# Two chained networks on one core: rounds of 384 + 384 rows and seven block products in both

## The chip, the cores and the metric

One core of a Trainium2 chip runs the whole program. The metric is device time in microseconds (us), launch to end. The engines are named as in the profile: PE (TensorE, matrix products), DVE (VectorE), ACT (ScalarE), POOL (GpSimd), SP (SyncE, which issues the DMAs).

## What is computed

Sparse attention, then two feed-forward networks one after the other. Weights arrive as 64-bit floats, the rest as 32-bit ones; the result has 1536 x 512 elements of 32 bits.

```python
# attention: 2 batches, 8 heads, 768 rows, 64 per head; a row sees 8 global and 96 local columns
attn = softmax(scale * q @ k.T + bias, kept columns only) @ v
x = attn as 1536 rows (2 batches of 768) x 512
h = x @ w_in1                                  # 512 x 2048
g = where(h >= 1, h, where(h <= -1, 0, (h + 1) ** 2 / 4))
x = g @ w_out1                                 # 2048 x 512
h = x @ w_in2
return maximum(0.01 * h, h) @ w_out2
```

## The kernel before

**Precision.** Each 32-bit operand of a product is kept as two parts, hi and lo, each in a format that PE takes at full rate. A product of two operands is three matmuls: hi hi, hi lo, lo hi. A copy (L253, L255) makes hi, a subtraction (L259, L261) makes lo.

**Weights.** Each network's 2048 hidden units are 16 chunks of 128. `job` (L460) brings one chunk of `w_in` (o = 0) or `w_out` (o = 1), 64 conversions in all: a DMA of 64-bit words, then s0 (L481, L483), s01 (L487), s1 (L491), s11 (L495), s2 (L499), s3 (L502), which build the 32-bit number, then s4 and s5, which split it into one of the weight places.

**Order of work.** Nothing is written in order by hand. `add` records an operation with its possible engines, its cost on each, a due time and what it waits for; `Schedule.run` (L96) then picks, for each engine, the ready operation that is due first, with buffers handed out from rings. The due times are the terms in `DUE` (L1138), one number for each kind of operation. Its rules count here: an operation that DVE or POOL may take goes to whichever is free, and neither begins an operation without PSUM while the other has one. PE runs what is ready, and before the first rows of the attention are done it runs dummy matmuls (L410).

**First network** (`step`, L779). The chunks go in three groups of 2, 7 and 7. The first group runs in six units of 256 rows, in between the attention, as soon as their rows are there. The others run in three units of 512 rows each. A step is one chunk for one unit: 12 matmuls for the hidden values (L796), the activation on ACT, DVE and POOL (L803 to L818, then hi and lo), 12 matmuls of the output (L858). The output's sums over the chunks of a group stay in PSUM, four banks for 512 rows; at the group's end they are copied into `part` in SBUF, or added to it (L897). After the last group the sums are split into hi and lo, in `x`, as the second network's input. `x_sums` (L941) makes four differences of its quarters, which the block products need.

**Second network** (`two`, L975). Chunks go in eight pairs. For the first 1024 rows, taken as 512 + 512, the hidden values of a pair are a product of 2 x 2 blocks, and they are done with seven block products (L990) instead of eight: two sums of weight blocks more (`sums`, L531, operations at L544), a copy of one bank into another, and two additions between banks (L1035, L1038), each of which stands between two products on PE. The last 512 rows are done directly (L1057). The output of each pair (L1072) is added to `part` bank by bank (L897, in the last pair L915), and then goes out.

PSUM has eight banks. Two word buffers (`wd_r`) and four to eight weight places for each kind let the conversions run ahead. `late` (L1090) frees the attention's buffers when it is done.

Of the kernel before, what the change touches and what calls it, by code (L numbers as in the profile page):

```python
# [205 lines left out]
def emit(tc, q, k, v, n_global, n_local, w_in1, w_out1, w_in2, w_out2, out, narrow):  # L206
# [63 lines left out]
    x = [const.tile([P, 2, KD, UM], F32R, name=f"x{u}") for u in range(NT // UM)]  # L270
    part = [const.tile([P, KD, UM], F32, name=f"part{r}") for r in range(2)] + [None]
# [5 lines left out]
    g_r = ring(const, "g", GN, [P, 2, UM], F32R)  # L277
    t_r = ring(const, "t", 2, [P, UM], F32)
# [36 lines left out]
    units = PASSES[0]  # L315
# [6 lines left out]
    for s, (m, g, u, f, first, last) in enumerate(seq):  # L322
        c = (u[1] - u[0]) * 10.15
        if m == 0 and g == 0 and u != units[-1]:
            after = quads(units[units.index(u) + 1])
            if first:
                seg = GROUPS[0] * c + len(after) * due_["ATT"]
                for i in after:
                    t_att[i] = z + seg * (i - after[0] + 0.5) / len(after)
            c += len(after) * due_["ATT"] / GROUPS[0]  # L330
        t_hid.append(z)
        z += c
    t_hid.append(z)

    NJ = KF // 2
    t_two = []
    z -= due_["TWO"]
    for j in range(NJ):
        for c in (90 * 227, 48 * 227):
            t_two.append(z)  # L340
            z += c
    t_two += [z, z + 48 * 227]
# [107 lines left out]
    for s, e in enumerate(seq):  # L450
        first_use.setdefault(e[0] * KF + e[3], s)
    NC = 2 * KF
    def due_of(c):
        return t_hid[first_use[c]] if c < KF else t_two[(c - KF) // 2 * 2]
# [5 lines left out]
    def job(c, o, prev):  # L460

        m, f = divmod(c, KF)
        due = due_of(c) + o * due_["OUTLAG"] - due_["JLEAD"] - (due_["JTWO"] if m and not o else 0)
# [55 lines left out]
        e2 = add(both(DM), s5, due + due_["s5"], [e1], gives=[] if m and not o else [Dd], late=LATE("s5"))  # L519
        if m and not o:  # L520
            words[f] = Dd, e2
            if f % 2:
                sums(f // 2, due)
# [7 lines left out]
    def sums(j, due):  # L531


        (Da, ea), (Db, eb) = words.pop(2 * j), words.pop(2 * j + 1)
# [41 lines left out]
    def quad(i):  # L576
# [8 lines left out]
        u, ti = divmod(Tt, UM // P)  # L585
# [111 lines left out]
        hi = x[u][:, 0, pp, ti * P:(ti + 1) * P]  # L697
        lo = x[u][:, 1, pp, ti * P:(ti + 1) * P]
# [70 lines left out]
    last_g = [len(GROUPS) - 1, NJ - 1]  # L769
    out_op, fin_op, x2_op, acc = {}, {}, {}, {}  # L770
    last_s = {(e[0] * KF + e[3]): s for s, e in enumerate(seq)}

# [6 lines left out]
    def step(s):  # L779
        m, g, u, f, first, last = seq[s]  # L780
        n = u[1] - u[0]
        r, c0 = divmod(u[0], UM)
        c = m * KF + f
# [3 lines left out]
        if s + 2 < NS:  # L787
            do = t_hid[s + 2] + per_ * due_["half"]
        else:
            do = d + 2.5 * per_  # L790
        wi, wo = w_t[c, 0], w_t[c, 1]
# [8 lines left out]
        def a1(e):  # L800
            t, h = Tt.tile[:, 0:n], Hb.tile[:, 0:n]
            if m == 0:
                A.activation(out=t, in_=h, func=AF.Relu, bias=half, scale=0.5)  # L803
            else:
                A.activation(out=t, in_=h, func=AF.Copy, scale=0.01)

        def a2a(e):

            t = Tt.tile[:, 0:n]
            if e == ACT:  # L810
                A.square(out=t, in_=t)  # L811
            else:
                (V if e == DVE else GP).tensor_tensor(out=t, in0=t, in1=t, op=ALU.mult)

        def a2(e):
            t, h = Tt.tile[:, 0:n], Hb.tile[:, 0:n]
            if m == 0:
                V.scalar_tensor_tensor(out=t, in0=h, scalar=1.0, in1=t, op0=ALU.max, op1=ALU.min)  # L818
            else:
                V.tensor_tensor(out=t, in0=t, in1=h, op=ALU.max)  # L820

        def a3(e):
            copy(e, Gt.tile[:, 0, 0:n], Tt.tile[:, 0:n])

        def a4(e):
            sub(e, Gt.tile[:, 1, 0:n], Tt.tile[:, 0:n], Gt.tile.bitcast(F32)[:, 0, 0:n])

        if m == 0:
            xs = [x_op.get(i) for i in range(u[0] // P * NQ, u[1] // P * NQ)]
        else:  # L830
            xs = [o for rr in range(u[0], u[1], 256) for o in x2_op[rr]]
        fin = s == last_s[c]
        o1 = add({PE: 12 * (n / 2.4 + 13.5)}, hid, d, [w_op[c, 0]] + (o_tb[1] if s < 3 else []) + xs + line("h"), takes=[Hs, Hb],
                 gives=[wi] if fin else [])
        o2 = add({ACT: act(n) + (107 if m == 0 else 0)}, a1, d + per_ / 2 + due_["a"], [o1] + line("a"), takes=[Tt])
        if m == 0:
            o2 = add({ACT: act(n, False), POOL: pool_tt(n), DVE: dve(n)}, a2a, d + per_ / 2 + 200 + due_["a"], [o2], late=LATE("a2"))
        o3 = add({DVE: dve(n)}, a2, d + per_ / 2 + 400 + due_["a"], [o2], gives=[Hb, Hs], ps=True)
        o4 = add({ACT: act(n, False), DVE: dve(n, True)}, a3, do - 2.4 * n - 500, [o3] + line("g"), takes=[Gt], late=LATE("a3"))
        chain.update(h=o1, a=o2, g=o4)  # L840
        o5 = add(both(n), a4, do - 1.3 * n - 300, [o4], gives=[Tt], late=LATE("a4"))

        nb = KD * n // 512 if m == 0 else n // P
        if first:
            acc[m, g, u] = [Slot(banks) for _ in range(nb)]
        bk = acc[m, g, u]
        nk = 512 // n if m == 0 else 1
        prev = out_op.get((m, g, u)) or [None] * nb
        now_ = []
        for cb in range(nb):  # L850
            def mm(e, cb=cb):
                o = bk[cb].tile
                for z in range(nk):
                    for a, b in ((0, 0), (0, 1), (1, 0)):
                        st, sp_ = (first and a + b + z == 0), (last and a == 1 and z == nk - 1)
                        if m == 0:
                            cc = cb * nk + z
                            T.matmul(out=o[:, z * n:(z + 1) * n], lhsT=wo.tile[:, a, cc * P:(cc + 1) * P],  # L858
                                     rhs=Gt.tile[:, b, 0:n], start=st, stop=sp_)
                        else:  # L860
                            T.matmul(out=o, lhsT=Gt.tile[:, b, cb * P:(cb + 1) * P], rhs=wo.tile[:, a, :],
                                     start=st, stop=sp_)
            pr = do + cb * 10
            gives = []
            if cb == nb - 1:
                gives = [Gt] + ([wo] if fin else [])
            o = add({PE: 3 * nk * (n / 2.4 + 13.5) if m == 0 else 681}, mm, pr, [o5, w_op[c, 1], prev[cb]] + now_[-1:] + line("o"), takes=[bk[cb]] if first else [],
                    gives=gives)
            now_.append(o)
        out_op[m, g, u] = now_  # L870
        if first:
            acc_op[m, g, u] = now_
        chain["o"] = now_[-1]
        if last:
            x2_op.setdefault(u[0], [])
            for cb in range(nb):
                finish(m, g, u, cb, bk[cb], now_[cb], do, nk)

    def finish(m, g, u, cb, B_, after, d, nk):
        n = u[1] - u[0]  # L880
        r, c0 = divmod(u[0], UM)
        if m == 0:
            sl = (slice(None), slice(cb * nk, (cb + 1) * nk), slice(c0, c0 + n))
        else:
            sl = (slice(None), c0 // P + cb)
        keys = [(m, rr, cb * nk + z) for z in range(nk) for rr in range(u[0], u[1], 256)] if m == 0 else \
            [(m, u[0] + cb * P, 0)]

        def ac():
            a = B_.tile  # L890
            return a.rearrange("p (k n) -> p k n", k=nk) if m == 0 else a

        def f0(e):
            copy(e, part[r][sl], ac())

        def f1(e):
            V.tensor_tensor(out=part[r][sl], in0=ac(), in1=part[r][sl], op=ALU.add)  # L897

        if g == 0:

            before = list(x2_op.get(("r", r), [])) if m else [o_late if r == 2 else None]
            o = add({ACT: act(512), DVE: dve(512)}, f0, d + 600 + cb, [after] + before, gives=[B_], ps=True)
            for kk in keys:
                fin_op[kk] = o
            return
        if m and g == last_g[m]:
# [377 lines left out]
```

## Time and profile before

| what | value |
|---|---|
| median of 3 runs | 612.18 us (612.14 to 613.44) |
| the profiled execution | 611.8 us |
| its span in the trace | 610.0 us |
| mean granted TensorE clock, share of full speed | 0.996 |
| PE busy | 601.5 us, 99% |
| DVE busy | 471.4 us, 77% |
| ACT busy | 351.6 us, 58% |
| POOL busy | 193.4 us, 32% |

The span is the stretch that the trace covers; the rest of the execution's time lies around it. Busy times are sums of instructions. A matmul's recorded duration includes its way through the array, so that neighbours overlap and a busy PE need not be at its peak; the distance from one start to the next tells more. DVE's recorded instructions overlap a little too.

### The profile page before, as it was taken

What the parts mean: (1) busy time and instruction counts of PE and PEld (TensorE: products, weight loads), DVE (VectorE), ACT (ScalarE), POOL (GpSimd) and SP (SyncE); (2) the same over time, 40 slices, a digit from 0 to 9 for tenths busy, and PEclk for the clock granted to TensorE, in tenths of its full rate; (3) what the DMA queues carried; (4) which work ended last, traced back from release to release, by engine and by line L of the source; (5) the groups of instructions that cost most, each with busy time, mean ns of one, the idle gap of its engine ahead of it and who ended that gap; (6) DMA issues with size and microseconds to landing.
All of it is one profiled execution on the core that took longest, in us unless ns stands there. A gap on an engine that the chain in (4) does not pass through costs nothing.

```text
span 610.0 us, 9623 instructions
## 1 busy us (share of the span) xinstructions
PE 601.5 (99%) x3398; PEld 506.4 (83%) x3398; DVE 471.4 (77%) x1044; ACT 351.6 (58%) x753; POOL 193.4 (32%) x244
## 2 busy tenths in 40 slices
PE   9999999999999999999999999999999999999995
PEld 7889999988888888888888888888888888788884
DVE  6999999999946897623488999249994889678663
ACT  6999999787534576434447457235652366336300
POOL 5666846223200121100111163004530484328200
PEclk9999999999999999999999999999999999999998
DMA  9857523334411334200012131201222113200014
GB/s 206 196 124 178 123 53 86 109 124 134 140 34 35 103 104 138 70 0 1 0 38 66 36 104 36 69 0 70 60 79 69 70 35 105 69 1 0 2 67 146
DMA packets 61809, 46.98 MB, mean 77 GB/s; under 512 B 39608, under 2 KB 56248, under 8 KB 61752
## 3 DMA queue, kind: packets, MB, share of 16 engines
q1 hardware_dynamic: 61744, 46.28, 26.8%
q8 instruction: 29, 0.48, 0.3%
q14 instruction: 28, 0.23, 0.2%
q10 hardware_dynamic: 8, 0.00, 0.0%
HBM read 43.12 MB, written 3.15 MB: 76 GB/s over the span
## 4 chain that ended last, share of the span: by engine, by line


## 5 line engine op out<-in xcount | busy, mean ns | idle before, releaser
L858 PE MATMUL bank<-g,w 128*128 128x512 f32 (+1 forms) x648 | 141.4, 367 | 0.0
L796 PE MATMUL bank<-x,w 128*128 128x512 f32 (+1 forms) x648 | 140.5, 367 | 0.0
L858 PEld LDWEIGHTS bank<-g,w 128*128 128x128 f32 x648 | 113.0, 188 | 20.1 <-issue 0.3
L796 PEld LDWEIGHTS bank<-x,w 128*128 128x128 f32 x648 | 112.3, 188 | 19.7 <-issue 0.2
L897 DVE TENSOR_TENSOR part<-bank,part 128x512 f32<-128x512 f32 x96 | 63.0, 683 | 34.4 <-PE bank L1072 28.3
L1072 PE MATMUL bank<-w,g 128*128 128x512 f32 x312 | 81.3, 389 | 0.0
L502 POOL TENSOR_TENSOR wd<-wd,wr 128x512 int32<-128x512 int32 x32 | 45.8, 1434 | 111.5 <-DVE wd L495 62.9
L253 ACT CAST g<-t 128x512 fp32r<-128x512 f32 (+1 forms) x67 | 39.5, 590 | 56.6 <-PE bank L858 30.5
L1072 PE MATMUL bank<-w,w 128*128 128x512 f32 x264 | 69.6, 389 | 0.0
L1072 PEld LDWEIGHTS bank<-w,g 128*128 128x128 f32 x312 | 58.6, 188 | 12.1
L1072 PEld LDWEIGHTS bank<-w,w 128*128 128x128 f32 x264 | 49.6, 188 | 10.3
L803 ACT ACTIVATE t<-bank,half 128x512 f32<-128x512 f32 (+1 forms) x54 | 34.6, 640 | 40.1 <-PE bank L796 37.0
L253 ACT CAST w<-wd 128x512 fp32r<-128x512 f32 x64 | 39.6, 621 | 27.0 <-DVE wd L502 9.2
L818 DVE SCALAR_TENSOR_TENSOR t<-bank,t 128x512 f32<-128x512 f32 (+1 forms) x54 | 33.7, 625 | 25.8 <-ACT t L811 25.5
L259 DVE TENSOR_TENSOR g<-t,g 128x512 fp32r<-128x512 f32 (+1 forms) x58 | 41.4, 718 | 15.1 <-ACT g L253 14.8
L499 ACT ACTIVATE wr<-raw 128x512 int32<-128x512 uint32 x64 | 43.1, 675 | 8.9 <-DVE wd L502 7.2
L495 DVE SCALAR_TENSOR_TENSOR wd<-raw,wd 128x512 int32<-128x512 int32 x64 | 47.6, 754 | 0.5
L990 PE MATMUL bank<-x,w 128*128 128x512 f32 x192 | 47.2, 389 | 0.0
L657 ACT ACTIVATE sm<-sm,st 128x256 f32<-128x256 f32 (+1 forms) x96 | 46.6, 499 | 0.4 <-DVE st L648 0.3
L672 POOL TENSOR_SCALAR sm<-sm,st 128x256 f32<-128x256 f32 (+1 forms) x78 | 37.8, 501 | 26.4 <-DVE st L663 21.2
L1057 PE MATMUL bank<-x,w 128*128 128x512 f32 x192 | 45.0, 389 | 0.0
L259 DVE TENSOR_TENSOR w<-wd,w 128x512 fp32r<-128x512 f32 x55 | 37.6, 695 | 7.7 <-ACT w L253 6.9
(117 smaller groups left out, 921.7 us busy)
## 6 DMA issues: line engine op xcount, KB each, us to landing
raw<-in_moe_w_in_dram SPq DMA_DIRECT2D x32, 512.0 KB, 3.8
raw<-in_moe_w_out_dram SPq DMA_DIRECT2D x32, 512.0 KB, 3.4
kd<-in_k_dram SPq DMA_DIRECT2D x24, 128.0 KB, 3.9
qd<-in_q_dram SPq DMA_DIRECT2D x24, 128.0 KB, 3.9
vd<-in_v_dram SPq DMA_DIRECT2D x12, 256.0 KB, 4.1
out_dram<-part SPq DMA_DIRECT2D x11, 256.0 KB, 2.2
out_dram<-part SPq DMA_DIRECT2D x2, 128.0 KB, 3.3
vg<-in_v_dram SPq DMA_DIRECT2D x2, 64.0 KB, 4.8
```

The costliest lines, as they stand in the source:

```text
L253: A.copy(out=out_, in_=in_)
L259: V.tensor_tensor(out=out_, in0=a, in1=b, op=ALU.subtract)
L495: V.scalar_tensor_tensor(out=Dd.tile, in0=hl()[0], scalar=-0x40000000, in1=Dd.tile, op0=ALU.bitwise_and, op1=ALU.bitwise_or)
L499: A.activation(out=Rr.tile, in_=hl()[1], func=AF.Copy, scale=2.0 ** -29)
L502: (V if e == DVE else GP).tensor_tensor(out=Dd.tile, in0=Dd.tile, in1=Rr.tile, op=ALU.add)
L657: A.activation(out=Sm.tile[:, a, 0:W], in_=Sm.tile[:, a, 0:W], func=AF.Exp, scale=-1.0, bias=St.tile[:, 0, a:a + 1], accum_out=St.tile[:, ...
L796: T.matmul(out=Hb.tile[:, 0:n], lhsT=wi.tile[:, a, kk * P:(kk + 1) * P], rhs=x[r][:, b, kk, c0:c0 + n], start=(kk == 0 and a + b == 0), st ...
L858: T.matmul(out=o[:, z * n:(z + 1) * n], lhsT=wo.tile[:, a, cc * P:(cc + 1) * P], rhs=Gt.tile[:, b, 0:n], start=st, stop=sp_)
L897: V.tensor_tensor(out=part[r][sl], in0=ac(), in1=part[r][sl], op=ALU.add)
L990: T.matmul(out=bank.tile, lhsT=w.tile[:, a, (2 * z + kk) * P:(2 * z + kk + 1) * P], rhs=xx()[:, b, kx + kk, :], start=st and kk == 0 and a ...
L1057: T.matmul(out=Hb.tile, lhsT=w.tile[:, a, kk * P:(kk + 1) * P], rhs=x[2][:, b, kk, :], start=(kk == 0 and a + b == 0), stop=(kk == KD - 1 ...
L1072: T.matmul(out=Bo.tile, lhsT=Gt[z, r].tile[:, b, cb * P:(cb + 1) * P], rhs=wo[z].tile[:, a, :], start=(z == 0 and a + b == 0), stop=(z == ...
```

## The change

Both networks now work in rounds of 768 rows, one batch, taken as 384 + 384. The first network keeps only its first two chunks (`SOLO`) as steps of 256 rows beside the attention. Its other 14 chunks are seven pairs: the first (`DIRECT`) is done directly, the other six in seven block products, as are all eight pairs of the second network, for both batches. Each pair's output is added to `part` by itself. For the first network's products the differences of quarters are made from the attention's output (`t_sums` with m = 0, which first adds hi and lo in two temporary tiles); weight sums are made for all pairs but the first. The weight places become 4 + 2 + 2 for `w_in` and 4 for `w_out`, the tiles of activations 7 of 384. All due times in `DUE` are other numbers. The diff's core:

```diff
-GROUPS = (2, 7, 7)
-SMALL = tuple((r, r + 256) for r in range(0, 1536, 256))
-LARGE = tuple((r, r + 512) for r in range(0, 1536, 512))
-PASSES = (SMALL, LARGE, LARGE)
+SOLO = 2
+PASSES = tuple((r, r + 256) for r in range(0, 1536, 256))
+UB, UH = 768, 384
 RING = 4
-MORE = 4
+MORE = 2
+MORE2 = 2
+MOREG = 3
+DIRECT = 1
...
+    seq = [(u, f) for u in PASSES for f in range(SOLO)]
...
+    PAIRS = [(0, f) for f in range(SOLO, KF, 2)] + [(1, f) for f in range(0, KF, 2)]
+    NJ = len(PAIRS)
...
+    def t_sums(m, q, kk, got, d):
...
+        if m == 0:
+            w0 = add(both(UB), lambda e: whole(e, kk), d - 200, [o_late] + got + x_rd[q] + t_last)
+            w2 = add(both(UB), lambda e: whole(e, k2), d - 100, [w0])
+            a0, b0, a2, b2 = [w0], [w0], [w2], [w2]
+        else:
+            a0, b0, a2, b2 = got
+        t1 = add(both(UH), c_((kk, 0), (kk, 1), (kk, 0)), d, a0 + b0)
+        t3 = add(both(UH), c_((kk, 1), (k2, 1), (kk, 1)), d + 100, [t1] + b2)
+        t2 = add(both(UH), c_((k2, 1), (k2, 1), (kk, 0)), d + 200, [t3])
+        t4 = add(both(UH), c_((k2, 0), (k2, 0), (k2, 1)), d + 300, [t2] + a2)
+        rd = x_rd[q] if m == 0 else []
+        us_ = [parts((kk, 0), lambda h: x[q][:, h, kk, hb[1]], UH, t1, 0, "t1", rd),
+               parts((kk, 1), lambda h: xt[q][1][:, h, kk], UH, t3, 100, "t3"),
+               parts((k2, 1), lambda h: xt[q][0][:, h, kk], UH, t2, 200, "t2"),
+               parts((k2, 0), lambda h: xt[q][2][:, h, kk], UH, t4, 300, "t4")]
...
+    def two(j, q):
+        m, f = PAIRS[j]
...
+                    o1 = add({PE: 2 * c6}, hid, dd, w1 + xs(y, 0) + (xs(y, 2) if m else []) + acc_op[units[-1]] + u_m.get("p", []), takes=[Hs, Hb])
...
+            p1 = add({PE: c6}, prod(Ba, wa, 0, xx(0, 0), True, False), d, w1 + xs(0, 0) + acc_op[units[-1]] + u_m.get("p", []),
                      takes=[Ba, Bb, Bc, Be] + Hs)
+            p5 = add({PE: c6}, prod(Be, wc, 1, xx(1, 0), True, True), d + n7, [p1] + wx_op[j] + t_of[m, q, "t1"])
...
+            p2 = add({PE: c6}, prod(Ba, wa, 1, xx(0, 2), False, True), d + 2 * n7, [p1, cp] + xs(0, 2))
+            p6 = add({PE: c6}, prod(Bb, wd_, 0, tt(0), False, False), d + 3 * n7, [cp] + wx_op[j] + t_of[m, q, "t2"])
+            cc = add({DVE: dve(UH)}, lambda e: V.tensor_tensor(out=t_(Bc), in0=t_(Bb), in1=S5.tile, op=ALU.add),
                      d + 3 * n7 + 1400 + due_["b0"], [p6, s5], ps=True)
+            p7 = add({PE: c6}, prod(Bb, wc, 0, tt(1), False, False), d + 4 * n7, [cc] + t_of[m, q, "t3"])
+            ce = add({DVE: dve(UH)}, lambda e: V.tensor_tensor(out=t_(Be), in0=t_(Bb), in1=S5.tile, op=ALU.add),
                      d + 4 * n7 + 1400 + due_["b0"], [p7, s5], gives=[S5], ps=True)
+            p3 = add({PE: c6}, prod(Bc, wd_, 1, xx(1, 2), False, True), d + 5 * n7, [cc] + xs(1, 2))
+            p4 = add({PE: c6}, prod(Bb, wb, 1, tt(2), False, True), d + 6 * n7, [ce] + t_of[m, q, "t4"])
...
+        if j < DIRECT:
+            direct()
         else:
+            blocks()
...
+        out_ = [(y, i) for i in (0, 2, 1, 3) for y in range(2)] if m == 0 else [(y, i) for y in range(2) for i in range(UH // P)]
...
+    def fin1(j, q, y, i, Bo, after, d):
+        p_ = part[q][:, i, hb[y]]
+
+        def f1(e):
+            V.tensor_tensor(out=p_, in0=Bo.tile[:, 0:UH], in1=p_, op=ALU.add)
+        o = add({DVE: dve(UH)}, f1, d + due_["f1" if j < J0 - 1 else "f2"], [after] + fin_op[0, q, i, y], gives=[Bo], ps=True)
...
+        if j == J0:
+            before = sum((t_of[1, q, a] for a in ("t1", "t2", "t3", "t4")), [])
+            fin_op[1, q, y, i] = add({ACT: act(DM), DVE: dve(DM)}, lambda e: copy(e, p_, Bo.tile), d + 600, [after] + before, gives=[Bo], ps=True)
+            return
...
+        xt.extend([pool.tile([P, 2, KD // 2, UH], F32R, name=f"xt{q}{i}") for i in range(3)] for q in range(2))
...
+        g_r.free += [pool.tile([P, 2, UH], F32R, name=f"g{GN + i}") for i in range(MOREG)]
```

A round of seven products is 42 matmuls of 384 columns, one of the direct pair 48. A round's output is 48 of 384 columns in the first network and 36 of 512 in the second.

## Rows read from the trace of the kernel before

**Rows 1.** The page: busy us, share, instructions; granted clock by slice.
```profile
PE 601.5 (99%) x3398; PEld 506.4 (83%) x3398; DVE 471.4 (77%) x1044; ACT 351.6 (58%) x753; POOL 193.4 (32%) x244
...
PEclk9999999999999999999999999999999999999998
```

**Rows 2.** The timeline of PE and its weight loads: start us, us, instructions.
```profile
595.82 2.88 PE L1072 MATMUL bank<-w,w 128*128 128x512 f32 x12
...
598.54 0.84 PE L1072 MATMUL bank<-w,g 128*128 128x512 f32 x3
...
124.60 3.04 PE L858 MATMUL bank<-g,w 128*128 128x256 f32 x24
127.47 0.86 PE L796 MATMUL bank<-x,w 128*128 128x512 f32 x3
...
99.88 1.15 PEld L796 LDWEIGHTS bank<-x,w 128*128 128x128 f32 x9
```

**Rows 3.** Groups of instructions by form, PE: count | busy us, mean ns.
```profile
L796 PE MATMUL bank<-x,w 128*128 128x512 f32 x504 | 121.0, 389 | 0.0
L858 PE MATMUL bank<-g,w 128*128 128x512 f32 x504 | 120.7, 389 | 0.0
...
L1072 PE MATMUL bank<-w,g 128*128 128x512 f32 x312 | 81.3, 389 | 0.0
L1072 PE MATMUL bank<-w,w 128*128 128x512 f32 x264 | 69.6, 389 | 0.0
...
L990 PE MATMUL bank<-x,w 128*128 128x512 f32 x192 | 47.2, 389 | 0.0
...
L1057 PE MATMUL bank<-x,w 128*128 128x512 f32 x192 | 45.0, 389 | 0.0
...
L990 PE MATMUL bank<-xt,w 128*128 128x512 f32 x144 | 36.7, 390 | 0.8 <-DVE bank L1035 0.8
```

**Rows 4.** Busy us by stage: PE, PEld, DVE, ACT, POOL; clock, DMA share, GB/s.
```profile
118.00:335.00 217.00, 217.00 (x992) 181.09 (x991) 156.89 (x268) 122.53 (x203) 33.94 (x30) 1.00 0.23 71
335.00:600.00 265.00, 264.23 (x1166) 218.56 (x1165) 201.66 (x335) 119.81 (x206) 91.85 (x77) 1.00 0.17 54
```

**Rows 5.** The timeline around the one wait: start us, us, instructions [idle before].
```profile
522.87 1.52 DVE L491 TENSOR_SCALAR wd<-wd 128x512 int32<-128x512 int32 x1
...
525.65 1.66 PE L990 MATMUL bank<-xt,w 128*128 128x512 f32 x6 [0.77 <-DVE bank L1035]
```

**Rows 6.** Groups by form, DVE and POOL: count | busy us, mean ns | idle before.
```profile
L897 DVE TENSOR_TENSOR part<-bank,part 128x512 f32<-128x512 f32 x96 | 63.0, 683 | 34.4 <-PE bank L1072 28.3 <-PE bank L858 5.9
L495 DVE SCALAR_TENSOR_TENSOR wd<-raw,wd 128x512 int32<-128x512 int32 x64 | 47.6, 754 | 0.5
...
L259 DVE TENSOR_TENSOR w<-wd,w 128x512 fp32r<-128x512 f32 x55 | 37.6, 695 | 7.7 <-ACT w L253 6.9
...
L491 DVE TENSOR_SCALAR wd<-wd 128x512 int32<-128x512 int32 x64 | 33.6, 536 | 0.4
...
L261 POOL TENSOR_TENSOR w<-wd,w 128x512 fp32r<-128x512 f32 x25 | 32.5, 1310 | 19.5 <-ACT w L253 15.0 <-DVE w L255 4.5
...
L502 DVE CUSTOM_DVE_ANT_0 wd<-wd,wr 128x1024 uint16<-128x1024 uint16 x32 | 22.7, 717 | 0.3
...
L487 DVE TENSOR_SCALAR wd<-wd 128x512 f32<-128x512 f32 x43 | 19.0, 453 | 2.3 <-ACT wd L481 1.9
...
L818 DVE SCALAR_TENSOR_TENSOR t<-bank,t 128x256 f32<-128x256 f32 x12 | 5.0, 414 | 0.0
```

**Rows 7.** Busy us in two full stretches, columns as in rows 4.
```profile
480.00:500.00 20.00, 20.00 (x89) 16.55 (x89) 18.04 (x33) 11.20 (x20) 14.84 (x13) 1.00 0.17 58
340.00:360.00 20.00, 20.00 (x90) 16.57 (x89) 19.71 (x35) 10.32 (x18) 7.13 (x6) 1.00 0.20 58
```

More of the change, by code (lines that the diff above doesn't have):

```diff
@@ L462, in job @@
         m, f = divmod(c, KF)
[L463 removed]
+        due = due_of(c) + o * due_["OUTLAG"] - due_["JLEAD"] - (due_["JTWO"] if c >= SOLO and not o else 0)
         R, Dd, Rr, W = Slot(raw), Slot(wd_r), Slot(wr_r), Slot(places[o])
@@ L518, in job @@
         chain["w", o] = e1
-        e2 = add(both(DM), s5, due + due_["s5"], [e1], gives=[] if m and not o else [Dd], late=LATE("s5"))
-        if m and not o:
-            words[f] = Dd, e2
+        e2 = add(both(DM), s5, due + due_["s5"], [e1], gives=[] if c >= SOLO + 2 * DIRECT and not o else [Dd], late=LATE("s5"))
+        if c >= SOLO + 2 * DIRECT and not o:
+            words[c] = Dd, e2
             if f % 2:
-                sums(f // 2, due)
+                sums((c - SOLO) // 2, due)
         add({NONE: 0}, lambda e: None, due - 6000, [c1, r], gives=[R])
@@ L839, in step @@
[L839 to L843, printed above, removed]
+        xs = [x_op.get(i) for i in range(u[0] // P * NQ, u[1] // P * NQ)]
+        fin = u == units[-1]
+        o1 = add({PE: 12 * (n / 2.4 + 13.5)}, hid, d, [w_op[f, 0]] + (o_tb[1] if s < 3 else []) + xs + line("h"), takes=[Hs, Hb],
+                 gives=[wi] if fin else [])
@@ L844, in step @@
+        x_rd[r].append(o1)
+        o5 = act_(0, n, t, h, Gt, Tt, [o1], [d + per_ / 2 + due_["a"], d + per_ / 2 + 200 + due_["a"], d + per_ / 2 + 400 + due_["a"],
+                                              do - 2.4 * n - 500, do - 1.3 * n - 300], [Hb, Hs], "a")
+        chain["h"] = o1
+        nb = KD * n // 512
         if first:
[L845 to L848, printed above, removed]
+            acc[u] = [Slot(banks) for _ in range(nb)]
@@ L866, in step @@
                 gives = [Gt] + ([wo] if fin else [])
[L867 to L870, printed above, removed]
+            now_.append(add({PE: 3 * nk * (n / 2.4 + 13.5)}, mm, do + cb * 10,
+                            [o5, w_op[f, 1], prev[cb]] + now_[-1:] + line("o"), takes=[bk[cb]] if first else [], gives=gives))
@@ L939, in emit @@
-    b_op, s_of = {}, {}
-    def x_sums(kk, d):
-        k2 = kk + KD // 2
+                sl = (slice(None), slice(cb * nk, (cb + 1) * nk), slice(c0, c0 + n))
+                o = add({ACT: act(512), DVE: dve(512)},
+                        lambda e, cb=cb, sl=sl: copy(e, part[r][sl], bk[cb].tile.rearrange("p (k n) -> p k n", k=nk)),
+                        do + 600 + cb, [now_[cb]], gives=[bk[cb]], ps=True)
+                for z in range(nk):
+                    for y in range(2):
+                        if c0 < (y + 1) * UH and c0 + n > y * UH:
+                            fin_op.setdefault((0, r, cb * nk + z, y), []).append(o)
@@ new lines, in act_, with a1, a2a, a2 @@
+    def act_(m, n, t, h, G_, Tt, after, dd, gives, kind):
+        def a1(e):
+            if m == 0:
+                A.activation(out=t(), in_=h(), func=AF.Relu, bias=half, scale=0.5)
+            elif e == ACT:
+                A.activation(out=t(), in_=h(), func=AF.Copy, scale=0.01)
+            else:
+                V.tensor_scalar(out=t(), in0=h(), scalar1=0.01, scalar2=None, op0=ALU.mult)
+        def a2a(e):
+            if e == ACT:
+                A.square(out=t(), in_=t())
+            else:
+                (V if e == DVE else GP).tensor_tensor(out=t(), in0=t(), in1=t(), op=ALU.mult)
+        def a2(e):
+            if m == 0:
+                V.scalar_tensor_tensor(out=t(), in0=h(), scalar=1.0, in1=t(), op0=ALU.max, op1=ALU.min)
+            else:
+                V.tensor_tensor(out=t(), in0=t(), in1=h(), op=ALU.max)
+        def a3(e):
+            copy(e, G_.tile[:, 0, 0:n], t())
+        def a4(e):
+            sub(e, G_.tile[:, 1, 0:n], t(), G_.tile.bitcast(F32)[:, 0, 0:n])
+        one = kind == "a"
+        o = add({ACT: act(n) + (107 if m == 0 else 0)}, a1, dd[0], after + (line("a") if one else []), takes=[Tt])
+        if one:
+            chain["a"] = o
+        if m == 0:
+            o = add({ACT: act(n, False), POOL: pool_tt(n), DVE: dve(n)}, a2a, dd[1], [o], late=LATE("a2"))
+        o = add({DVE: dve(n)}, a2, dd[2], [o], gives=gives, ps=True)
+        o = add({ACT: act(n, False), DVE: dve(n, True)}, a3, dd[3], [o] + (line("g") if one else []), takes=[G_], late=LATE(kind + "3"))
+        if one:
+            chain["g"] = o
+        return add(both(n), a4, dd[4], [o], gives=[Tt], late=LATE(kind + "4"))
@@ new lines, in two, with mm @@
+        for no, (y, i) in enumerate(out_):
+            Bo = Slot(banks)
+            def mm(e, y=y, i=i, Bo=Bo):
+                for z in range(2):
+                    for a, b in ((0, 0), (0, 1), (1, 0)):
+                        g_, w_ = Gt[z, y].tile, wo[z].tile
+                        kw = dict(start=(z == 0 and a + b == 0), stop=(z == 1 and a == 1))
+                        if m == 0:
+                            T.matmul(out=t_(Bo), lhsT=w_[:, a, i * P:(i + 1) * P], rhs=g_[:, b], **kw)
+                        else:
+                            T.matmul(out=Bo.tile, lhsT=g_[:, b, i * P:(i + 1) * P], rhs=w_[:, a, :], **kw)
+            dd = dn + no * (d2 - dn) / len(out_) + due_["bo"]
+            o = add({PE: c6 if m == 0 else 6 * 226.8}, mm, dd, [g_op[0, y], g_op[1, y], w_op[ca, 1], w_op[cb_, 1]], takes=[Bo])
+            lm[y].append(o)
+            (fin1 if m == 0 else fin2)(j, q, y, i, Bo, o, dd)
```

400 lines of the change are left out of this document (160 added, 240 removed).

## The prediction

> **What bounds the kernel now.** I read the page's busy shares first. TensorE is busy for 99% of a span of 610.0 us, DVE for 77%, POOL for 32%, and TensorE's granted clock is full in every slice but the last [rows 1]. A busy PE on the page only says that matmuls follow each other, so I went to their spacing. Twelve 512-column matmuls begin at 595.82 and the next group at 598.54: 2.72 / 12 = 226.7 ns each. Twenty-four 256-column ones begin at 124.60 and the next group at 127.47: 119.6 ns [rows 2]. The counts by shape give 504 + 504 + 312 + 264 + 192 + 144 + 192 = 2,112 matmuls of 512 columns [rows 3]; with the 288 of 256 columns that the loops of the first two chunks make (12 steps of 24), that is 2,112 x 0.2267 + 288 x 0.1196 = 513.2 us at these spacings. From 118 us to 600 us PE is busy for 217.00 of 217 and 264.23 of 265 us [rows 4]; the missing 0.77 us is one wait, for a DVE addition in the seven-product chain [rows 5]. So behind the attention PE's columns are the time, and the elementwise engines stay just ahead of it. Both halves of the change act on this: fewer columns, and more elementwise work.
>
> **PE, the sum.** Kept: the attention, and the two solo chunks (288 of 256 columns). Removed: the 2,112. Added in the first network: the direct pair, 2 rounds x (48 + 48) = 192 matmuls of 384 columns, and six pairs in seven products, 6 x 2 x (42 + 48) = 1,080. In the second: 8 x 2 x 42 = 672 of 384, and 8 x 2 x 36 = 576 of 512. Together 1,944 of 384 columns and 576 of 512. No 384 stands in the trace; between the two spacings the line is (226.7 - 119.6) / 256 = 0.418 ns a column, so 384 columns take 173.2 ns. Sum: 1,944 x 0.1732 + 576 x 0.2267 = 336.7 + 130.6 = 467.3 us for 478.8, a saving of **11.5 us**. The bounds of the price are narrow: the weight loads could set the pace of shorter matmuls, yet nine loads for 256 columns pass in 1.15 us, 128 ns apart [rows 2], under 173. At 175 ns the saving is 8.0 us.
>
> The rows put 13 ns on each matmul over its column time (226.7 - 512 x 0.418). The Trainium skill (TensorE: Matmul & The Clock Gate, section Back-to-back issue gap) states N / 2.4 + 2.5 ns for an isolated gap when warm; by it the estimate is 162.5 and 215.8 ns and the saving 15.6 us. The spacing of 226.7 ns disagrees, and the sum goes by the rows.
>
> **The elementwise prices.** DVE takes 683 ns for 512 elements of a bank and 414 for 256, so I take 0.55 us for 384 and 0.68 + 0.27 = 0.95 for 768. POOL takes 1310 ns where DVE takes 695: 1.9 us of POOL are one of DVE [rows 6]. Below, a "DVE-us" is work that DVE or POOL must do, counted at DVE's price.
> - Sums pair by pair: 7 x 2 x 8 = 112 additions of 384 for 24 of 512: 61.6 - 16.4 = +45.2. They read PSUM, and no POOL instruction of this kernel does.
> - The additions between banks, two for each round of seven products: 12 rounds in the first network, +13.2; in the second 16 for 8 at 0.69 twice, 17.6 - 11.0 = +6.6.
> - Sums of weights for six pairs: 6 x (4 x 0.42 + 2 x 0.70) = +18.5.
> - Sums of the attention's rows: four times 2 x 0.95 + 8 x 0.55 = +25.2.
> - Splitting and summing the second network's input: 44 pieces of 384 for 26 of 512, +6.5; the activations' shorter pieces, about +5.
> Together +120. By stages: the first network did 156.89 + 33.94 / 1.9 = 175 DVE-us [rows 4]; it gets 45.2 + 13.2 + 18.5 + 25.2 and half of the last line, 108, so 283 in (192 + 1,080) x 0.1732 = 220.3 us of PE: **1.28 DVE-us per us**. The second gets 18: 201.66 + 91.85 / 1.9 + 18 = 268 in its 247 us, 1.08.
>
> **What the engines can do.** In the stretches where DVE was full and PE did not wait, it and POOL together did (18.04 + 14.84 / 1.9) / 20 = 1.29 and (19.71 + 7.13 / 1.9) / 20 = 1.17 per us [rows 7]. So the first network goes from slack to the edge, and it does not go evenly.
> - Its first 65 us (the direct pair and the next) hold: activations 16 x 1.1 = 17.6, evictions 24 x 0.55 = 13.2, the sums of rows 25.2, two pairs of weights, bank additions 2.2, leftovers of the solo chunks about 3. A pair of weights is four conversions of 0.45 + 0.54 + 0.75 + 0.72 + 0.70 [rows 6] and its sums, 15.7. That is 93, less 5 for the words of two conversions that can be ready before (two word buffers). At 1.29 the engines do 84, so PE waits 4 / 1.29 = **3.2 us**; at 1.17, 10 us. I take 3.2: a third of this work reads PSUM and can run beside POOL, which is nearer to the faster row. Here the waits should be of the second pair's products, for the sums of rows or for the weights.
> - At the handover to the second network, two rounds (31 us) hold 8.8 + 2.2 + 8.8 + 6.6 + 17.6 = 44: at 1.29, 2.9 us short; at 1.17, 6.4. At the handover before (340 to 360) PE did not wait [rows 7], with the 512 rows of the third unit as cover; now the cover is one round. I take the middle between none and 2.9, **1.5 us**.
> - The first pair waits until the last solo unit has begun its outputs. Before, long groups of 512 columns filled that place (two windows of them around 124.60). A gap there, at most some 6 us if DVE is full, gives the elementwise engines that time, so it pays down the 3.2 and is not added. The same holds for more waits like that 0.77 in 28 rounds instead of 8 (2.7 us).
> Edits costed at nothing: the 64 weight loads are the same and needed more evenly, with DMA busy 0.23 of the first network's stage; ACT had 94 of 217 us free there [rows 4], and takes copies and casts; the output's last rows leave as before. The attention's instructions stay, and only their due times differ; that can go either way by some 2 us.
>
> **Forecast.** -11.5 + 3.2 + 1.5 = -6.8 us. The profiled execution took 611.8 us, with 610.0 of span; the median of the three is 612.18, 0.4 above. From the median: **605.4 us**.
>
> **Rivals.**
> - *PE alone decides.* The order keeps the products fed and no new wait shows: 612.2 - 11.5 = 600.7. For it: one wait of 0.77 us in 482 now. Against: the first network's slack is gone. Chance 0.24.
> - *DVE and POOL become the bound of the first network.* What decides is the rate: below 283 / (220.3 + 11.5) = 1.22 DVE-us per us the waits eat the whole saving. At 1.17 the stage lasts 242 us instead of 220.3, and the kernel 612.2 - 11.5 + 21.6 = 622; at 1.20, 616. For it: the 1.17 row, and that a DVE instruction without PSUM stretches beside POOL: the 536-ns mask takes 1.52 us at 522.87 [rows 5, 6]. Against: the 1.29 row, with more POOL work in it. Chance 0.20. The Trainium skill (SBUF — State Buffer, section Who interferes with whom) has DVE and POOL share one port pair as an exclusive lock, with which such work never overlaps; the stretched row agrees.
> - *Loads pace the 384 columns*, at 188 ns or more: 1,944 x 0.015 = 29 us, 630. Rows 2 speak against it. Chance 0.01.
> - *The change does less than it says:* the direct pair is one of seven, so six pairs save. This is counted.
>
> **How the numbers follow.** Between the first two rivals lies the forecast, 602 to 610, chance 0.47; from there to no change, 0.08. What a measurement can tell from no change is about 0.2%, 611.0 to 613.4. Faster 0.71, same 0.08, slower 0.21. The range leaves out a tenth on each side: down to 600, the case without waits, and up to 616, the second rival at 1.20.
>
> **What would show it.** Matmuls of 384 columns 173 ns apart; 1,944 and 576 of them; DVE over 90% and POOL over 40% from 120 to 340 us; PE gaps of some microseconds between 150 and 190 us and again near 340, whose releasers are DVE or POOL on sums, weights or banks. Wrong would be: gaps spread over every round of the first network (the second rival), no gaps at all (the first), or an attention phase that ends much earlier or later.

## The result: 616.7 us where 605.4 was forecast, and the profile after

The kernel after takes **616.74 us** (median of 10 runs, 614.74 to 617.69), the kernel before in the same runs 612.53. The ratio to the kernel before is **1.0059, interval 1.0044 to 1.0074**: slower by 0.6%, outside the range of 600 to 616. The profiled execution took 616.41 us, with a span of 614.5.

The page of the kernel after, its busy line and granted clock, against [rows 1]:

```profile
PE 597.5 (97%) x3802; PEld 553.9 (90%) x3802; DVE 547.0 (89%) x1242; ACT 385.3 (63%) x898; POOL 290.6 (47%) x335
...
PEclk9999999999999999999999999999999999999998
```

The clock is full, so it takes no part. PE's busy time fell by 4.0 us while the span grew by 4.5: PE stood idle for 17 us instead of 8.5. DVE has 76 us more, POOL 97. PE's groups by form, against [rows 3] (count | busy us, mean ns | idle before):

```profile
L1043 PE MATMUL bank<-w,g 128*128 128x512 f32 x576 | 139.0, 392 | 0.2 <-DVE part L1080 0.2
L944 PE MATMUL bank<-x,w 128*128 128x384 f32 x672 | 129.2, 335 | 1.5 <-ACT bank L254 1.5
L1041 PE MATMUL bank<-g,w 128*128 128x384 f32 x672 | 124.5, 335 | 0.6 <-DVE t L855 0.4
L944 PE MATMUL bank<-xt,w 128*128 128x384 f32 x504 | 102.2, 337 | 6.6 <-DVE bank L1007 5.8 <-DVE bank L1010 0.7
```

With 96 more of the direct pair (L981) these are the 576 and 1,944 of the prediction. The columns were saved. What PE waited for is in its list of waits (us in total, times, longest):

```profile
PE bank L944 <- DVE bank L1007: 5.8, 7, 1.3
PE bank L944 <- ACT bank L254: 1.5, 2, 1.1
...
PE bank L944 <- DVE bank L1010: 0.7, 1, 0.7
```

What matters is their kind. There is not one stretch in which work is short; there are single waits of about 1 us, most of them for L1007, one of the two additions between banks that stand between two products. To place them I took, for every matmul, the time to the next one's start less the steady spacing of its shape (226.7 ns for 512 columns, 173.4 for 384), summed by stretch. The first column also holds what follows the last product. There, and ahead of 120 us, where dummy matmuls and waits for data mix, only differences between kernels count.

| us lost by PE | to 120 us | 120 to 320 | 320 to 365 | from 365 on | sum |
|---|---|---|---|---|---|
| before | 22.4 | 0.1 | 0.0 | 1.0 | 23.5 |
| after | 23.3 | 4.5 | 4.9 | 6.4 | 39.1 |

So the change saved 11.1 us of columns (2,112 x 226.7 - 1,944 x 173.4 - 576 x 226.7 ns) and lost 15.6 us, +4.5 as the spans say. Behind 120 us the loss is 12 gaps over 0.3 us (10.7 us together), smaller ones (about 3), and some 2 us of slightly wider spacing.

**One gap in detail.** The timelines of DVE, POOL and PE in the kernel after, around 175 us (start us, us):

```profile
172.62 0.55 DVE L898 TENSOR_TENSOR tmp<-tmp 128x384 f32<-128x384 f32 x1
173.09 0.68 DVE L492 SCALAR_TENSOR_TENSOR wd<-raw,wd 128x512 int32<-128x512 int32 x1
173.69 0.42 DVE L488 TENSOR_SCALAR wd<-wd 128x512 int32<-128x512 int32 x1
174.02 1.65 DVE L260 TENSOR_TENSOR xt<-tmp,xt 128x384 fp32r<-128x384 f32 x1
175.59 0.68 DVE L492 SCALAR_TENSOR_TENSOR wd<-raw,wd 128x512 int32<-128x512 int32 x1
176.19 0.55 DVE L1007 TENSOR_TENSOR bank<-bank,s 128x384 f32<-128x384 f32 x1
...
173.84 1.41 POOL L499 TENSOR_TENSOR wd<-wd,wr 128x512 int32<-128x512 int32 x1 [2.50 <-DVE wd L492]
...
173.24 1.20 PE L944 MATMUL bank<-xt,w 128*128 128x384 f32 x6
174.28 1.21 PE L1041 MATMUL bank<-g,w 128*128 128x384 f32 x6
176.80 1.33 PE L944 MATMUL bank<-xt,w 128*128 128x384 f32 x6 [1.32 <-DVE bank L1007]
```

POOL's L499 began 0.18 us ahead of DVE's L260. That subtraction, 0.55 us a moment earlier at 172.15, now lasts 1.65, to 0.42 us behind POOL's end; the bank addition behind it begins 1.1 us later, and PE, which has six products of 173 ns (1.04 us) in between, begins the next ones 2.52 us later. In the plan this cannot happen, since there neither engine begins an operation without PSUM while the other has one. On the chip only the order on each engine is kept: POOL was free and its data had come, and it began ahead of a DVE instruction that the plan has first. Seven of the twelve gaps, those at 175, 249, 329, 397, 476, 517 and 567 us, follow a DVE instruction of SBUF operands that was stretched by over 1 us beside POOL; the one at 356 follows two stretched by 0.8. Behind 120 us, twelve DVE instructions of SBUF operands lost over 1 us against the usual time of their form, and near seven of them a gap of PE over 0.3 us begins; in the kernel before it is eight, and one gap. The other four gaps are at 289 and 446 us (0.5 each), 349 (0.6) and 361 (1.3). The last, at the handover, waits for a copy of a bank on ACT:

```profile
362.43 1.32 PE L944 MATMUL bank<-x,w 128*128 128x384 f32 x6 [1.11 <-ACT bank L254]
```

The Trainium skill (SBUF — State Buffer, section Who interferes with whom) says that a DVE instruction with two SBUF inputs contends with a GpSimd instruction that reads SBUF, that their shared pair of ports is an exclusive lock, and that the order of issue decides who is blocked. The rows agree: DVE came second and was held for 1.10 us of POOL's 1.41; no DVE instruction with a bank among its operands ran over 0.02 us longer than usual behind 120 us, and DVE's bank addition keeps 0.55. The trace shows the hold itself, too. Behind 120 us, 70 DVE instructions of SBUF operands ran over 0.1 us longer than usual; each began while a POOL instruction was running, and each ended 0.13 us less than its usual time behind the end of POOL's, within 0.01 us. So a held DVE instruction does nearly all its work after POOL's end, and what it loses is what POOL still has to do.

### The profile page after: what moved, and what is told of

Read it like the earlier page. It is cut to its first block, busy times and chain, and to the rows that moved or that the text cites. A ratio compares the mean times of both kernels' runs of the same rounds, so it can differ in the third digit from the quotient of the medians.

```text
span 614.5 us, 10896 instructions
## 1 busy us (share of the span) xinstructions
PE 597.5 (97%) x3802; PEld 553.9 (90%) x3802; DVE 547.0 (89%) x1242; ACT 385.3 (63%) x898; POOL 290.6 (47%) x335
## 4 chain that ended last, share of the span: by engine, by line
## 5 line engine op out<-in xcount | busy, mean ns | idle before, releaser
L1043 PE MATMUL bank<-w,g 128*128 128x512 f32 x576 | 139.0, 392 | 0.2 <-DVE part L1080 0.2
L944 PE MATMUL bank<-x,w 128*128 128x384 f32 x672 | 129.2, 335 | 1.5 <-ACT bank L254 1.5
L1043 PEld LDWEIGHTS bank<-w,g 128*128 128x128 f32 x576 | 107.3, 188 | 21.5 <-DVE part L1080 0.7
L1041 PE MATMUL bank<-g,w 128*128 128x384 f32 x672 | 124.5, 335 | 0.6 <-DVE t L855 0.4
L944 PEld LDWEIGHTS bank<-x,w 128*128 128x128 f32 x672 | 117.9, 188 | 4.3 <-ACT bank L254 2.1
L499 POOL TENSOR_TENSOR wd<-wd,wr 128x512 int32<-128x512 int32 x48 | 71.6, 1494 | 94.8 <-DVE wd L492 82.3
L944 PE MATMUL bank<-xt,w 128*128 128x384 f32 x504 | 102.2, 337 | 6.6 <-DVE bank L1007 5.8
L944 PEld LDWEIGHTS bank<-xt,w 128*128 128x128 f32 x504 | 88.2, 188 | 11.7 <-DVE bank L1007 9.1
L262 POOL TENSOR_TENSOR w<-wd,w 128x512 fp32r<-128x512 f32 x50 | 67.3, 1352 | 50.1 <-ACT w L254 24.5
L254 ACT CAST g<-t 128x384 fp32r<-128x384 f32 (+1 forms) x113 | 55.6, 505 | 35.9 <-PE bank L1043 10.7
L1058 DVE TENSOR_TENSOR part<-bank,part 128x384 f32<-128x384 f32 x112 | 57.7, 551 | 4.8 <-PE bank L1041 4.3
L260 DVE TENSOR_TENSOR g<-t,g 128x384 fp32r<-128x384 f32 (+1 forms) x93 | 59.7, 670 | 0.9 <-ACT g L254 0.4
```

The costliest lines, as they stand in the source:

```text
L254: A.copy(out=out_, in_=in_)
L260: V.tensor_tensor(out=out_, in0=a, in1=b, op=ALU.subtract)
L262: GP.tensor_tensor(out=out_, in0=a, in1=b, op=ALU.subtract)
L499: (V if e == DVE else GP).tensor_tensor(out=Dd.tile, in0=Dd.tile, in1=Rr.tile, op=ALU.add)
L944: T.matmul(out=bank.tile[:, 0:UH], lhsT=w.tile[:, a, (2 * z + kk) * P:(2 * z + kk + 1) * P], rhs=xx(b, kk), start=st and kk == 0 and a + b ...
L1041: T.matmul(out=t_(Bo), lhsT=w_[:, a, i * P:(i + 1) * P], rhs=g_[:, b], **kw)
```

## The experiments

Three theories. **Port**: POOL runs ahead of the plan, holds DVE, and a bank addition comes late. **Volume** (the prediction's second rival): DVE and POOL simply have too much to do. **Chain**: with 384 columns the way from a product over an addition to the next product is too long by itself.

### Taking work away: e1, e2, e3

e1 cuts POOL's instructions behind the attention to 32 columns, where their target had been written before. e2 cuts DVE's additions of outputs. e3 cuts POOL, DVE and ACT alike, in the way of e1. Orders and counts stay; outputs lack the columns left out.

Parts of the diffs, first of e1 and e3, then of e2:

```diff
+            if self.cut and self.sch.now > CUT_FROM and key in self.full:
+                for k in ("out", "in_", "in0", "in1"):
+                    if k in kw and len(kw[k].shape) == 2 and kw[k].shape[-1] > CUT_N:
+                        kw[k] = kw[k][:, 0:CUT_N]
...
-            V.tensor_tensor(out=p_, in0=Bo.tile[:, 0:UH], in1=p_, op=ALU.add)
+            V.tensor_tensor(out=p_[:, 0:32], in0=Bo.tile[:, 0:32], in1=p_[:, 0:32], op=ALU.add)
```

> The changed kernel with the same instructions in the same order on every engine, but once the attention is done POOL's instructions take 32 columns instead of 256 to 768 (where their target has been written before), so parts of the weights, the sums and the splits are left out; DVE's, ACT's and PE's instructions keep their sizes. In the trace of the changed kernel PE's waits of about 1 us each follow a DVE instruction without PSUM that is stretched by some 1.2 us while a POOL instruction runs (at 174.02 a difference of 384 takes 1.65 us instead of 0.55, and the bank addition behind it on DVE comes 1.3 us late for PE). Theory 'port': the stretches are the cause; without POOL's time they go, and with them most of the 16 us of waits (614.5 of span less 598.5): time 601 to 606. Rival 'volume': DVE has simply too much of its own to do (17 to 20 of 20 us busy); its instructions are all still there, so PE waits as before: 612 or more. Rival 'chain': rounds of 384 rows leave PE too little other work while a bank addition is made, whatever DVE does: 614 or more.

> The changed kernel, same order, but DVE's additions of the outputs to the sums in SBUF take 32 columns instead of 384 (112 of them) and 512 (84): the sums of the outputs are left out. They read PSUM. DVE loses about 112 x 0.37 + 84 x 0.50 = 83 us of work; POOL and the stretches beside it stay. Theory 'port': the stretches still come, but DVE catches up sooner, so a part of the waits goes: 605 to 611. Rival 'volume': all waits go, 601 to 604. Rival 'chain': no change, 614 or more.

> The changed kernel, same order, but after the attention all of POOL's, DVE's and ACT's instructions take 32 columns (where their target has been written before): nearly all elementwise work is left out. What is left is PE with its order. All theories: no wait of PE behind the attention, so the columns alone decide: 612.5 - 11.5 = 601 us, within 2 us. If it stays above 604, the sum over the columns was wrong, and not the waits.

Measured: e1 605.24 (604.93 to 607.42; ratio 0.9883, 0.9867 to 0.9900), e2 611.34 (0.9987, 0.9976 to 0.9998), e3 603.54 (0.9855, 0.9838 to 0.9871). The busy lines of e1 and e2:

```profile
PE 595.9 (98%) x3802; PEld 556.7 (92%) x3802; DVE 515.5 (85%) x1242; ACT 382.3 (63%) x898; POOL 139.3 (23%) x335
```

```profile
PE 596.2 (98%) x3802; PEld 554.4 (91%) x3802; DVE 486.0 (80%) x1242; ACT 384.0 (63%) x898; POOL 289.6 (47%) x335
```

e2 takes 77 us of additions from DVE, the engine that is full (their instructions take 34.1 us for 111.1; there were 72 of 512 columns, not the 84 of the expectation), and wins 5.4 us; it ends 0.3 above the interval of the port theory and 7 above that of the volume. DVE's busy time falls by 61 us only, in part because its stretches grow from 37.9 us to 48.7. e1 takes nothing from DVE and wins 11.5; DVE's busy time falls by 31.5 us all the same, because its instructions are no longer stretched (behind 120 us the stretches sum up to 37.9 us in the kernel after, to 2.2 in e1). Volume as defined here falls with e2, chain with e1; but e1 also takes work from POOL, so DVE and POOL together having too much to do is settled only by e4. e3 is PE's floor, 2.5 us above what was expected: its loss is 24.3 us up to 120 us and 2.1 behind.

### Keeping POOL behind DVE: e4, and the same in the kernel before: e6

All work stays, and so does the order on every engine. Each POOL instruction now also waits for the DVE instruction without PSUM that stands last before it in the plan:

```diff
+                    had = len(traced)
                     o.fn(e)
+                    if e == DVE and not o.ps:
+                        last = [i for i in traced[had:] if i.engine == mybir.EngineType.DVE][-1]
+                    if e == POOL and last is not None:
+                        first = [i for i in traced[had:] if i.engine == mybir.EngineType.Pool][0]
+                        self.tc.add_manual_dep(
+                            first, last.name,
+                            mybir.DependencyInfo(mybir.DependencyClass.Sync, mybir.DependencyReason.DATA),
+                            reason="planned order")
```

> The kernel after with all its work and the same order on every engine; only, each instruction of POOL now also waits for the end of the DVE instruction that reads SBUF and stands last before it in the planned order, so that POOL cannot run ahead into it. Port theory (a POOL instruction that runs ahead holds a DVE instruction of SBUF operands for 1.1 us, and the bank addition queued behind it comes late): the stretched instructions (L260 at 1.65 in place of 0.55 us) go, and most of the 15.6 us of waits that the kernel after has more than the kernel before: 600 to 607 us, PE's waits for DVE banks below 2 us. Volume theory (DVE and POOL have too much to do): nothing to gain, and POOL loses time in waits: 616 to 622. Chain theory (the two bank additions between two groups of matmuls are too long for 384 columns): 614 to 618.

> The kernel before with the same edit as e4_pool_waits (POOL waits for the DVE instruction planned ahead of it), its order unchanged. In its two networks PE loses only about 1 us to waits, so under the port theory there is little to win and the price of the waits themselves shows: 611 to 613.5, ratio 0.998 to 1.002. If keeping POOL back were a gain of its own, whatever the change (fewer stretches in the attention): below 609. If the added waits cost POOL time that somebody needs: above 614.

e4: **605.95 us** (605.30 to 607.43), ratio to before **0.9898, 0.9883 to 0.9914**, 10.8 us below the kernel after by the medians (11.0 by the spans of the profiled executions, 9.9 by the ratios to the kernel before). Its busy line, and PE's waits in e4 (L957 is L944 of the kernel after, all lines 13 on; the first is the dummy matmuls' start at the very beginning):

```profile
PE 594.6 (99%) x3802; PEld 554.8 (92%) x3802; DVE 538.8 (89%) x1242; ACT 385.2 (64%) x898; POOL 271.2 (45%) x335
...
PE bank L420 <- DVE zero L424: 1.1, 1, 1.1
PE bank L957 <- ACT bank L267: 1.0, 1, 1.0
PE bank L1054 <- DVE t L868: 0.2, 1, 0.2
```

No wait for a bank addition is left. The wait for the copy on ACT at the handover is: it is the gap at 361 us of the kernel after, and so no collision of this kind.

```profile
355.64 1.34 PE L957 MATMUL bank<-x,w 128*128 128x384 f32 x6 [1.03 <-ACT bank L267]
```

The same place as above in e4, DVE, POOL and PE:

```profile
171.44 0.55 DVE L911 TENSOR_TENSOR tmp<-tmp 128x384 f32<-128x384 f32 x1
171.91 0.68 DVE L505 SCALAR_TENSOR_TENSOR wd<-raw,wd 128x512 int32<-128x512 int32 x1
172.51 0.42 DVE L501 TENSOR_SCALAR wd<-wd 128x512 int32<-128x512 int32 x1
172.85 0.55 DVE L273 TENSOR_TENSOR xt<-tmp,xt 128x384 fp32r<-128x384 f32 x1
173.32 0.68 DVE L505 SCALAR_TENSOR_TENSOR wd<-raw,wd 128x512 int32<-128x512 int32 x1
173.92 0.56 DVE L1020 TENSOR_TENSOR bank<-bank,s 128x384 f32<-128x384 f32 x1
...
174.08 2.54 POOL L512 TENSOR_TENSOR wd<-wd,wr 128x512 int32<-128x512 int32 x2 [3.91 <-DVE wd L505]
...
173.46 1.21 PE L1054 MATMUL bank<-g,w 128*128 128x384 f32 x6
174.53 1.33 PE L957 MATMUL bank<-xt,w 128*128 128x384 f32 x6
```

The same six DVE instructions, with 2.48 us from the first to the bank addition instead of 3.57, and the next six products 1.07 us behind the last instead of 2.52. POOL does nothing earlier; it waits 3.91 us and nobody misses it. One thing was expected wrongly: stretched instructions did not go. Against the 70 of the kernel after, 71 DVE instructions of SBUF operands ran over 0.1 us longer than usual in e4. But none loses more than 1 us now. By the edit they can only be instructions that the plan has behind POOL's: they got there early and wait their turn, and no wait of PE follows.

e6: 610.62 us (0.9968, 0.9956 to 0.9981), 0.4 below its interval. The one wait of the kernel before [rows 5] comes from the same kind of collision, twice in a row: L502 and then L491 (at 522.87) each lose 1.10 us beside a POOL instruction that began earlier.

```profile
521.17 1.78 DVE L502 CUSTOM_DVE_ANT_0 wd<-wd,wr 128x1024 uint16<-128x1024 uint16 x1
...
520.86 1.54 POOL L261 TENSOR_TENSOR g<-t,g 128x512 fp32r<-128x512 f32 x1 [1.41 <-ACT g L253]
522.36 1.74 POOL L261 TENSOR_TENSOR w<-t,w 128x512 fp32r<-128x512 f32 x1
```

In e6, with all lines 13 on, the first of these two POOL instructions begins 1.5 us later, behind both of DVE's:

```profile
521.20 0.68 DVE L515 CUSTOM_DVE_ANT_0 wd<-wd,wr 128x1024 uint16<-128x1024 uint16 x1
521.80 0.42 DVE L504 TENSOR_SCALAR wd<-wd 128x512 int32<-128x512 int32 x1
...
522.37 1.29 POOL L274 TENSOR_TENSOR g<-t,g 128x512 fp32r<-128x512 f32 x1 [2.89 <-ACT s L266]
```

PE loses 0.1 us behind 120 us instead of 1.1. That is half of the 2.0 us that e6 wins by the medians; where the rest comes from, these runs do not show. With POOL kept back in both kernels, the change is worth 610.62 - 605.95 = 4.7 us.

### Another order: e5

Only the constants in `DUE` are other numbers, so that the same work is planned in another order.

```diff
-DUE = {'t3': 103594.0, 't4': 5672.0, 'x1': -60928.0,
+DUE = {'t3': 35159.0, 't4': 6850.0, 'x1': -395733.0,
...
```

> The kernel after with other due times alone (the one line of constants from which the order is planned): every instruction is the same, the order is another, chosen so that DVE's bank additions have more room where POOL runs ahead. Port theory: the waits come from which POOL instruction stands beside which DVE instruction, so another order changes them: 602 to 609. Volume theory: DVE and POOL have the same sum of work, the time stays at 614 to 619. Chain theory: 614 to 618.

610.67 us (0.9966, 0.9953 to 0.9979), 6.1 below the kernel after and 1.7 above the interval of the port theory. The volume is the same, so volume falls again; but choosing an order wins about half of what keeping it wins, and PE still loses 2.5 us between 160 and 200 us. Most of that is one collision, the longest of all runs, with a POOL sum of 768 elements:

```profile
160.79 2.19 DVE L260 TENSOR_TENSOR xt<-tmp,xt 128x384 fp32r<-128x384 f32 x1
...
160.55 2.02 POOL L893 TENSOR_TENSOR tmp<-x 128x768 f32<-128x768 f32 x1 [4.16 <-DVE xt L260]
```

### Half of the waits: e7, e8

The condition on POOL's waits gets `and now < 335000.0` (e7) or `and now >= 335000.0` (e8).

> e4_pool_waits with the added waits of POOL only up to the handover to the second network (planned time below 335 us). By PE's spacing the kernel after loses 4.2 us more than e4 between 120 and 320 us, 1.5 between 320 and 360, and 5.7 behind. If each collision costs where it happens: 616.7 - 4.2 to 5.7, so 610.5 to 613. If the first network's stalls put the engines behind for all that follows: 608 or less. If the first network has nothing to do with it: 616 or more.

> The other half: the added waits of POOL only from the handover on. If each collision costs where it happens: 616.7 - 5.7 to 7.2, so 609 to 611.5, and with e7 the two gains sum up to e4's 10.8. If the first network's stalls put the engines behind for the rest: 614 or more.

e7: 610.45 us (0.9959, 0.9944 to 0.9974), at the lower end of the first case (0.05 below it). e8: 612.36 (0.9998, 0.9989 to 1.0007), 0.9 above its interval. The gains are 6.3 and 4.4, together 10.7 against e4's 10.8 (by the spans of the profiled executions 5.9 and 3.7, against 11.0, so the close match is in part luck). By place, from the spacing of PE as above; PE's products stand in the same order in all these kernels, and each column holds the same products as that of the kernel after:

| us lost by PE | to 120 us | 120 to 320 | 320 to 365 | from 365 on | sum |
|---|---|---|---|---|---|
| after | 23.3 | 4.5 | 4.9 | 6.4 | 39.1 |
| e4, all waits | 23.5 | 0.4 | 2.0 | 2.2 | 28.1 |
| e7, first half | 24.0 | 0.3 | 3.4 | 5.6 | 33.3 |
| e8, second half | 24.1 | 5.3 | 3.8 | 2.3 | 35.5 |

Each half clears its own stretches: a collision costs where it happens. In e7 the gaps of the second half stand in front of the same products as in the kernel after, with the same lengths (1.33, 0.92, 0.40, 0.76 and 0.91 us); only the 0.49 at 446 us is gone. e8 keeps the four long gaps of the first network (1.46, 1.03, 0.55, 1.02) and gets one more (0.64 at 145 us), and from 365 us on it loses 0.1 us more than e4. Against the kernel after it wins 5.2 us behind 320 us, and loses 0.8 between 120 and 320 and 0.8 in the first column, which is its miss.

### The opposite wait: e9

DVE's instructions without PSUM wait for POOL's instruction planned ahead of them; POOL stays free.

```diff
+                    if e == POOL:
+                        last = [i for i in traced[had:] if i.engine == mybir.EngineType.Pool][-1]
+                    if e == DVE and not o.ps and last is not None:
+                        first = [i for i in traced[had:] if i.engine == mybir.EngineType.DVE][0]
```

> The kernel after with the opposite wait: each DVE instruction that reads SBUF waits for the end of the POOL instruction that stands last before it in the planned order; POOL is as free as in the kernel after. Port theory: the loss comes from DVE being held up, so this can win nothing and adds holds: 616 to 624, PE's waits for DVE banks not below those of the kernel after. If keeping the planned order in any form were what helps (fewer instructions side by side): 604 to 612.

618.18 us (617.15 to 618.47; 1.0084, 1.0066 to 1.0103). PE's waits for L1007, here L1020, are hardly shorter than in the kernel after (5.2 us for 5.8), and on DVE's timeline the stretch of the detailed gap is still there. Its busy line, the wait and the stretch:

```profile
PE 599.3 (97%) x3802; PEld 554.0 (90%) x3802; DVE 527.6 (86%) x1242; ACT 386.0 (63%) x898; POOL 291.5 (47%) x335
...
PE bank L957 <- DVE bank L1020: 5.2, 7, 1.5
...
175.10 1.64 DVE L273 TENSOR_TENSOR xt<-tmp,xt 128x384 fp32r<-128x384 f32 x1
```

DVE has only 20 stretched instructions now, for 70, and 19 us less busy time, and the kernel is no faster; in e4 nearly all stretches stayed, and it is. So neither waits nor fewer stretches as such help, but keeping POOL from getting in ahead of a DVE instruction that the plan has first.

## Why the prediction was wrong, point by point

- **Columns, -11.5.** Right: 1,944 and 576 matmuls, and -11.1 at the measured spacing. In the first network of e4 a 384 comes every 173 ns (median). In the second network, where rounds mix 384 and 512, the spacing is a little wider, which costs some 2 us in all and stood in no term.
- **The failed step** is the last sentence on the handover's neighbours: "The same holds for more waits like that 0.77 in 28 rounds instead of 8 (2.7 us)". They were costed at nothing, as time that pays down a shortage. But a shortage of volume is paid down by any pause, and a collision is not: it comes from who begins first, once per event. e4 shows the term's size, **10.8 us** in place of 0. Even the 2.7 was too small: it scaled one event by rounds, while DVE had gone from slack to full, and there were more long stretches (twelve for eight) and far more gaps behind them (seven for one). That the lack of slack is what turns more of them into gaps is argued from this and from e2, whose eleven long stretches and 77 us less of work went with 5.4 us less time. In the kernel after DVE is busy without a break in such stretches as this one (the same columns as in rows 4):

```profile
340.00:360.00 20.00, 18.39 (x104) 17.62 (x103) 19.98 (x39) 11.50 (x26) 10.15 (x10) 1.00 0.00 1
```

- **Early shortage, +3.2.** Near in size and place (2.7 us between 120 and 200 us), by luck, for the cause was wrong. In e4, with the same work, 0.1 us is lost there. Those 2.7 us belong to the 10.8.
- **Handover, +1.5.** With POOL kept back, e4 loses 2.0 us there (320 to 365 us of the kernel after), 1.2 of it in the one gap for ACT's copy, which shrinks to 0.4 only in e3; the kernel after loses 4.9 in the same products. The term is about right, the rest is collisions.
- **Attention, 0 within 2.** 0.9 us in the kernel after, 1.1 in e4 and up to 1.9 in most experiments; 3.7 in e1, whose profiled execution was the slowest of its four (607.42 us, the others 604.93 to 605.47).
- **The sum.** Put right, it is -11.1 for columns, +11.0 for collisions (39.1 - 28.1 in the tables), +2.0 for the handover and about +2.6 for the attention, the wider spacing and small gaps, less the kernel before's own wait: +4.5. Without the collisions it is -6.5, as e4's span of 603.5 has it against 610.0, where -6.8 was forecast. That the forecast of 605.4 fits e4 is luck: its 3.2 us of shortage are 0.1 there, and the 2.6 that fill their place stood in no term. Two slips in the working change nothing. The second network's 18 DVE-us hold the last line whole, though half of it had gone to the first network (12.4, and 1.06 per us for 1.08); and 4 / 1.29 is 3.1.
- **The second rival** named 616 for a rate of 1.20 DVE-us per us. The number came, the mechanism did not: the waits go on through the second network, and e4 runs at such a rate with no wait for a bank addition. Its windows (busy us of PE, PEld, DVE, ACT, POOL; then clock):

```profile
120.00:185.00 65.00, 65.00 (x388) 64.82 (x387) 62.26 (x119) 43.32 (x89) 27.38 (x27) 1.00 0.15 50
185.00:340.00 155.00, 155.00 (x894) 154.50 (x893) 146.50 (x284) 102.14 (x201) 76.07 (x74) 1.00 0.23 75
```

By the prediction's own formula these are (62.26 + 27.38 / 1.9) / 65 = 1.18 and (146.50 + 76.07 / 1.9) / 155 = 1.20 with PE busy throughout. So the threshold of 1.22 did not hold: it rests on 283 DVE-us of demand, and in e4 the first network's products take 224.4 us with 269, stretches included. The stretched row was in hand ([rows 5]), and was read as a rate, in favour of this rival, instead of as a delay in front of a bank addition.
- **Loads**, 630: did not happen.
- **The signs** that the prediction named for itself came in the kernel after, in its window from 120 to 340 us (DVE 94%, POOL 49%), and so did gaps near 175 and 340 to 360 us. They could not tell a shortage from collisions, since both go with a full DVE:

```profile
120.00:340.00 220.00, 216.46 (x1250) 214.02 (x1249) 206.55 (x391) 143.03 (x280) 108.51 (x98) 1.00 0.22 68
```

## What to carry to other kernels

When a schedule assumes that two engines take turns, look whether anything on the chip enforces it; where nothing does, a wait on the engine that has slack (here POOL) cost nothing here and keeps the other's instructions on time. Price a stretch as a delay to what is queued behind it, by events and not by rates: holding POOL back won 10.8 us, taking 77 us of work from the full engine 5.4. And where an engine has become full, look for collisions that had been harmless: here eight long stretches gave one gap before the change, and twelve gave seven after it.

## What was not expected of the hardware

One more semaphore wait on POOL's instructions cost nothing that shows: the kernel before, too, became faster by 0.3% with it (e6). POOL's own busy time fell with it, from 290.6 to 271.2 us in e4, with all its work. A stretch has no size of its own: it is what POOL still has to do, less 0.13 us, so that it reached 1.14 us in the kernels before and after and 1.64 beside POOL's instruction of 2.02 us in e5. And busy time misled: e1 lowered DVE's by 31.5 us without taking any work from it.
